# Weights converted from float64 at the start of a fused attention and feed-forward kernel: w_out and w3 in shared units, and the last output in two parts

## The chip, the cores and the metric

The kernel runs on one core of a Trainium2 chip. The metric is the device time of one execution in microseconds; the kernel before was run three times for it, and once more with the profiler on.

## What is computed

Random-feature attention over (8, 8, 576, 64) float32 inputs is followed by a bilinear feed-forward layer whose four weights are float64:

```
proj = x @ omega.T ;  phi(x) = exp(proj - |x|^2/2 - max) / sqrt(m)      # m = 128 features
kv = phi(k).T @ v ;  z = sum(phi(k)) ;  x = (phi(q) @ kv) / (phi(q) @ z)
out = ((x @ w1) * (x @ w2)) @ w3 @ w_out        # x (4608, 512), w1, w2 (512, 1024), w3 (1024, 1024), w_out (1024, 512)
```

## The kernel before, in words

**Chunks.** The 4608 tokens are 36 chunks of 128. Each chunk of keys and of queries is loaded, projected on the features by TensorE (`features`, L323 in float32 for the first key and query chunks, L330 with operands split in two float16 parts for the later ones), reduced to a maximum per head by VectorE (L342, `nm`), and put through exp by ScalarE (L354 or L357). The products of keys and values are summed by batch (`kv_batch`, L447), queries are attended (`q_attend`, L476), and the normalized rows `x` are transposed by a DMA. `gate` (L733) forms x @ w1 and x @ w2 in quarters of a group of chunks, multiplies them and splits the product in two float16 parts; `project_out` (L762 to L767) multiplies with W = w3 @ w_out, which is formed once at the start, scales by ScalarE (L766) and stores a chunk by one DMA of 256 KB (L767).

**Weights.** float64 weights come as pairs of 32-bit words and are converted on the chip in units of 1 MB, 128 partitions x 1024 numbers (`from_float64`). A unit is a list of five stages: `fetch` (a DMA into one of three raw buffers, L568), `magnitude` (ScalarE takes Abs of the upper words, L577), `bits` (VectorE makes float32 out of both words in four passes, L584 to L592), a product, and `keep`. For the first unit each stage works on two halves. Unit kinds, by their letter in `ORDER`: `o` is two blocks of 128 rows of w_out; `W` holds 256 columns of w3 transposed for 512 rows, and its product (L670) runs over four blocks j of w_out, for two output blocks k, in two PSUM banks; `keep` copies them to `Wb` (L685), or, for the second half of the rows, adds to it (L683). `1` and `2` are parts of w1 and w2, with column sums (L618, L622); `a`, `b` and `S` scale and split what is complete. A product of 128x128 by 128x512 in float32 is two records in the trace.

**What sets the order.** `ORDER` lists 25 units. Stage s of unit n is issued at tick n + SKEW[s] (0, 1, 2, 3, 5), and PER says how many ticks fall in a slot; the steps of the chunks (norms, scales, splits, k, q, attend, kv) are put in slots by tables of offsets (KOFF, QOFF, VB, KV_LAG and others). Each instruction's place in that list is its rank; the framework's scheduler takes ready instructions by rank when it builds the queues of the engines, and `early(kind, ...)` moves a step's rank forward by PR[kind] places (back, if negative). So a line of code that comes earlier isn't always first on its engine. `tc.issue_after(converted[-1])` puts an edge between the last pass of one unit and the passes of the next on VectorE; `converted[1]` also holds back the maxima of the first key chunk, and `converted[0]` and `converted[1]` some loads of v and q.

**Buffers.** TensorE writes to two PSUM pools: two double banks for projections, kv and nu (`banks`), and four single banks (`bank_m`) shared by the weight products, the column sums, the norms (L194), the gate and the output. Three raw buffers of 1 MB and two for magnitudes hold the units in work.

Of the kernel before, what the change touches and what calls it, by code (L numbers as in the profile page):

```python
# [9 lines left out]
F32 = mybir.dt.float32  # L10
# [9 lines left out]
P = 128  # L20
# [5 lines left out]
PASSES = ((0, 0), (0, 1), (1, 0))  # L26

F64_LEAST, F64_TOP = 2.0**-15, float.fromhex("0x1.dffffep+16")

# [3 lines left out]
QS = "a"  # L33
VS = "a"
WS = "a"
EH = 'aaaaaddadaaadaaaaaaaaaa'
EL = 'ddppddpdpddpppppppppppppppp'
QH = 'aaaaaaddd'
QL = 'ddpdppppppppppp'
DQ = '101110010000000000000000000'  # L40
QF = 6
KF = 11
VF = 9
V_ACT = 1
PR = {'vscale': 100, 'norm': 400, 'split': 100, 'bits': -100, 'x': 50}
START = 1
MS = 0
WADD = 1
FQ = 's'
T0 = 1  # L50
CH = 1
KFIRST = 0
QD = 1
OM1 = 0
DK = '1111111110000000000000'


ORDER = 'ooW1W1aW2W2booWWWW11a22bS'
SKEW = [0, 1, 2, 3, 5]

PER = [3, 1, 0, 1, 0, 1, 1, 0, 1, 0, 1, 1, 0, 1, 1, 0, 0, 1, 1, 1, 1, 1, 1, 1, 0, 3, 0, 1, 1, 1, 1, 1, 2]
# [13 lines left out]
OM_AT = 0  # L75
K_BEHIND = 1
RAW64_BUFS = 3
O_BUFS = 2
# [11 lines left out]
def tile_favor_attention_then_bilinear_ffn(  # L90
# [19 lines left out]
    nc = tc.nc  # L110
    NCH = qT.shape[0]
# [9 lines left out]
    DO = wo.shape[1] // 2  # L121
# [24 lines left out]
    def bank_m(name):  # L146
        return ps_m.tile([P, 512], F32, tag="pm", name=name)
# [398 lines left out]
    converted = []  # L546
# [8 lines left out]
    def from_float64(new, src, name, cuts=1):  # L555

        st = {}
        pieces = [slice(k, k + 1024 // cuts) for k in range(0, 1024, 1024 // cuts)]

        def fetch():  # L560
            at = st["at"] = raw_at.pop(0)
            nfetch[0] += 1
            raw = arena[:, at : at + 4].bitcast(U32).rearrange("p b i -> p (b i)")

            raw = raw.rearrange("p (j i) -> p j i", j=src.shape[1])
            step = src.shape[1] // cuts
            for k in range(0, src.shape[1], step):
                {'a': nc.scalar, 's': nc.sync, 'p': nc.gpsimd}[pick(FQ, nfetch[0])].dma_start(raw[:, k : k + step], src[:, k : k + step])  # L568
            st["raw"] = raw.rearrange("p j i -> p (j i)").rearrange("p (i t) -> p i t", t=2)

        def magnitude():

            at = st["mag"] = mag_at.pop(0)
            st["g"] = arena[:, at : at + 2].rearrange("p b i -> p (b i)")
            st["dst"] = new()
            for a in pieces:
                nc.scalar.activation(st["g"][:, a], st["raw"][:, a, 1].bitcast(F32), AF.Abs)  # L577

        def words():
            for a in pieces:  # L580
                g, dst = st["g"][:, a], st["dst"][:, a].bitcast(U32)
                top, low = st["raw"][:, a, 1], st["raw"][:, a, 0]

                nc.vector.tensor_scalar(g, g, F64_TOP, F64_LEAST, ALU.min, ALU.max)  # L584
# [71 lines left out]
    def W_block(n):  # L656

        i, j0 = n * 2 % NF, n * 2 // NF * HALF
        at = HALF + n % 2 * 2
        w3c = guest[:, at : at + 2].rearrange("p b i -> p (b i)")  # L660
        pss = []

        def product():
            w = w3c.rearrange("p (j i) -> p j i", j=HALF)
            for k in range(2):
                ps = bank_m(f"wp_{n}_{k}")
                if j0 and not WADD:
# [88 lines left out]
    def project_out(c):  # L756
        sc = oscs[:, c : c + 1]
        nc.vector.tensor_scalar(sc, pts[c], pts[c], kap, ALU.mult, ALU.mult)
        ps = bank_m(f"o_{c}")
        mm = [(f, a, b) for f in range(NF) for a, b in PASSES]  # L760
        for i, (f, a, b) in enumerate(mm):
            nc.tensor.matmul(ps, hs[c, f][0][:, a], W[f][:, b], start=i == 0, stop=i == len(mm) - 1)  # L762
        for f in range(NF):
            used(hs[c, f][1])
        o = mo.tile([P, DO], F32, tag="o", name=f"o_{c}", bufs=O_BUFS)
        nc.scalar.mul(o, ps, sc)  # L766
        nc.sync.dma_start(out[c * P : (c + 1) * P, :], o)  # L767


    LEAD = 5  # L770
# [20 lines left out]
    def unit(keep=0):  # L791
# [7 lines left out]


    make = {
        "o": wo_load,
        "W": W_block,
        "1": lambda i: w12_load(0, i),
        "2": lambda i: w12_load(1, i),
        "a": lambda i: [early("wsplit", lambda: w12_split(0, i))],
# [12 lines left out]
    for n, u in enumerate(units[:RAW64_BUFS]):  # L819
        u[0]()  # L820
        u[0] = None
        if START and n < 2:
            load(kT, n, "k", nc.scalar)
# [150 lines left out]
```

## Time and profile before

| | us |
|---|---|
| median of 3 runs (816.82 to 817.98) | 817.17 |
| the profiled execution's own time | 817.29 |
| its span in the profile | 815.5 |
| PE busy | 776.2 |
| DVE busy | 544.9 |
| ACT busy | 443.6 |
| POOL busy | 213.4 |

PE is TensorE, PEld its weight loads, DVE VectorE, ACT ScalarE, POOL GpSimd, SP the queue that issues most DMAs. The span is what the profiler saw of the program on the core; the time of a run has 1.8 us around it. A difference of 1 us is 0.12% of the time.

### The profile page before, as it was taken

The numbers are of one execution on the slowest core, as the hardware profiler recorded it, in microseconds if no ns is written. First come the engines' busy times: TensorE is split into PE (matmuls) and PEld (weight loads), VectorE is DVE, ScalarE is ACT, GpSimd is POOL, SyncE is SP. The second block draws the span as 40 slices with busy tenths as digits, with TensorE's granted clock in tenths as the row PEclk, the third lists the DMA queues.
The fourth block names the chain that finished last, engine by engine and source line by source line (L and its number), as shares of the span: only waits on it lengthen the run. The fifth ranks groups of instructions, "written<-read, shape, count | busy, mean of one in ns | idle before, by whom it ended". The sixth has DMA issues, their size and how long they took to land.

```text
span 815.5 us, 19863 instructions
## 1 busy us (share of the span) xinstructions
PE 776.2 (95%) x8320; PEld 578.9 (71%) x8320; DVE 544.9 (67%) x1045; ACT 443.6 (54%) x793; POOL 213.4 (26%) x208
## 2 busy tenths in 40 slices
PE   2998898998979999999999999999999999999998
PEld 2456557967758777777777778777777777777773
DVE  6898979867898686677767665686758654552210
ACT  4896667855766557566655555466545433332221
POOL 0000101121434243333332334333423321231110
PEclk9999999999999999999999999999999999999999
DMA  8787854233544364335434435254433342231101
GB/s 297 268 289 229 228 164 118 54 53 85 137 107 89 80 151 96 81 103 131 92 79 121 101 80 103 66 132 92 100 59 87 69 79 67 53 59 46 39 14 39
DMA packets 142537, 88.38 MB, mean 108 GB/s; under 512 B 116720, under 2 KB 116848, under 8 KB 142448
## 3 DMA queue, kind: packets, MB, share of 16 engines
q1 hardware_dynamic: 142160, 86.60, 42.0%
q8 instruction: 65, 1.06, 0.5%
q10 hardware_dynamic: 288, 0.52, 0.2%
q14 instruction: 24, 0.20, 0.1%
HBM read 49.35 MB, written 9.44 MB: 72 GB/s over the span
## 4 chain that ended last, share of the span: by engine, by line
PE 84%; DVE 6%; DMA 4%; ACT 3%; issue 2%; SPq 0%; ACTq 0%; DVEq 0%
PE ab L733 42%; PE o L762 21%; PE wp L670 7%; PE kvp L447 5%; PE nu L476 3%; PE qpj L330 2%; PE kpj L330 2%; DMA kraw<-kT 1%; DMA arena<-wo 1%; DVE nm L342 1%; DVE khl L175 1%; DMA arena<-w 1%; ACT qe L354 1%; DVE w12b L592 1%; DVE arena L589 1%
## 5 line engine op out<-in xcount | busy, mean ns | idle before, releaser
L733 PE MATMUL ab<-xT,w12b 128*128 128x256 f16 (+1 forms) x3840 | 393.9, 263 | 3.3 <-DMA xT<-xhl 2.7
L733 PEld LDWEIGHTS <-w12b 128*128 128x128 f16 x3840 | 341.8, 98 | 42.6 <-issue 3.2
L762 PE MATMUL o<-Wb,arena 128*128 128x512 f16 x864 | 192.4, 379 | 1.9 <-ACT asb L742 1.9
L748 POOL TENSOR_TENSOR arena<-asb,arena 128x512 f16<-128x512 f32 x72 | 84.7, 1176 | 279.8 <-ACT arena L747 272.7
L762 PEld LDWEIGHTS <-arena 128*128 128x128 f16 x864 | 82.1, 98 | 95.9 <-issue 2.0
L366 POOL TENSOR_TENSOR eq<-qe,eq 128x1024 f16<-128x1024 f32 x33 | 70.3, 2130 | 147.4 <-DVE eq L161 80.6
L743 DVE TENSOR_TENSOR asb<-ab,asb 128x512 f32<-128x512 f32 x72 | 49.5, 687 | 85.3 <-PE ab L733 71.9
L747 ACT CAST arena<-asb 128x512 f16<-128x512 f32 x72 | 44.3, 616 | 97.7 <-DVE asb L743 97.7
L366 POOL TENSOR_TENSOR ek<-ke,ek 128x1024 f16<-128x1024 f32 x25 | 53.3, 2130 | 87.7 <-ACT ek L163 87.1
L670 PE MATMUL wp<-w12b 128*128 128x512 f32 x128 | 62.9, 647 | 3.3 <-DVE w12b L592 3.3
L357 ACT ACTIVATE qe<-qe,ln_e,es 128x1024 f32<-128x1024 f32 x29 | 35.9, 1239 | 44.9 <-DVE qe L356 44.9
L742 ACT ACTIVATE asb<-ab 128x512 f32<-128x512 f32 x72 | 41.9, 582 | 20.1 <-PE ab L733 15.1
L357 ACT ACTIVATE ke<-ke,ln_e,es 128x1024 f32<-128x1024 f32 x25 | 31.0, 1240 | 39.5 <-DVE ke L356 39.4
L670 PEld LDWEIGHTS wp<-w12b 128*128 128x128 f32 x128 | 25.6, 207 | 34.2 <-issue 29.7
L175 DVE SCALAR_TENSOR_TENSOR qhl<-qraw,s,qhl 128x512 f16<-128x512 f32 x30 | 26.9, 898 | 33.2 <-ACT qhl L172 33.2
L513 DVE SCALAR_TENSOR_TENSOR xhl<-xs,p2r,xhl 128x512 f16<-128x512 f32 x36 | 28.3, 787 | 27.7 <-ACT xhl L512 27.5
L161 DVE CAST eq<-qe 128x1024 f16<-128x1024 f32 x30 | 21.2, 708 | 37.6 <-ACT qe L357 37.0
L766 ACT ACTIVATE o<-o,oscs 128x512 f32<-128x512 f32 x36 | 24.5, 680 | 37.8 <-PE o L762 37.8
L342 DVE TENSOR_REDUCE nm<-kpj 128x8 f32<-128x1024 f32 x36 | 43.8, 1219 | 1.2 <-PE kpj L330 0.6
L342 DVE TENSOR_REDUCE nm<-qpj 128x8 f32<-128x1024 f32 x36 | 43.8, 1217 | 0.2
L189 ACT ACTIVATE junk_q<-qraw 128x512 bf16<-128x512 f32 x30 | 18.8, 627 | 45.5 <-DMA qraw<-qT 45.5
L447 PE MATMUL kvp<-vhl,ek 128*128 128x65 f16 (+1 forms) x880 | 41.6, 208 | 1.2 <-DVE qe L356 1.0
(124 smaller groups left out, 923.9 us busy)
## 6 DMA issues: line engine op xcount, KB each, us to landing
vraw<-v SPq DMA_DIRECT2D x36, 256.0 KB, 3.8
qraw<-qT SPq DMA_DIRECT2D x36, 256.0 KB, 2.8
out<-o SPq DMA_DIRECT2D x36, 256.0 KB, 2.7
kraw<-kT SPq DMA_DIRECT2D x34, 256.0 KB, 3.1
arena<-w3T SPq DMA_DIRECT2D x8, 1024.0 KB, 5.3
arena<-w SPq DMA_DIRECT2D x8, 1024.0 KB, 5.9
arena<-wo SPq DMA_DIRECT2D x3, 1024.0 KB, 7.2
eqT<-eq SPq DMA_TRANSPOSE x72, 3.1
```

The lines of the kernel that those rows point to most:

```text
L175: nc.vector.scalar_tensor_tensor(lo, src, s, hi, ALU.mult, ALU.subtract)
L342: nc.vector.tensor_reduce(nm, pj, AX.X, ALU.max, negate=True)
L357: nc.scalar.activation(e, e, AF.Exp, scale=es, bias=ln_e)
L366: (nc.vector if lo == "d" else nc.gpsimd).tensor_tensor(t[:, 1], e, t[:, 0], ALU.subtract)
L447: nc.tensor.matmul(ps[:, h // 4, h % 4], x, y, start=n == 0, stop=n == len(mm) - 1)
L670: nc.tensor.matmul(ps, w[:, j, k * P : (k + 1) * P], guest[:, j], start=j == (0 if WADD else j0), stop=j == HALF - 1,)
L733: nc.tensor.matmul(ps[:, k], w12[m][i][cc][:, a, r * P : (r + 1) * P], x[:, b, cc, off : off + T], start=j == 0, stop=j == len(mm) - 1,)
L742: nc.scalar.mul(asb, ab[0], 2.0**-37)
L743: nc.vector.tensor_tensor(asb, ab[1], asb, ALU.mult)
L747: nc.scalar.copy(h[:, 0], asb)
L748: nc.gpsimd.tensor_tensor(h[:, 1], asb, h[:, 0], ALU.subtract)
L762: nc.tensor.matmul(ps, hs[c, f][0][:, a], W[f][:, b], start=i == 0, stop=i == len(mm) - 1)
```

## The change

The first four units are of a new kind, `F`. Unit j holds block j of w_out (512 KB) and, of w3 transposed, the same block of 128 rows with 512 columns (512 KB), fetched by two DMAs. Its product is four matmuls, one into each of the four single banks, opened by j = 0 and closed by j = 3; the `keep` of the last unit copies all four banks to Wb by ScalarE. So the four F units do what two `o` and two `W` units did. `ORDER` has the same number of units; the first two parts of w1 come one or two places later.

The first unit (CV 'C') is converted in another way: ScalarE scales the upper words (Copy) and makes the top three bits of the lower word out of one of its bytes (Identity), and VectorE needs three passes instead of four. CH = 4 makes each of the first four units wait on VectorE for the one before (it was 1: none).

The last chunk's output is formed in two halves of 256 columns, each with its own bank, matmuls, scaling and DMA (TAIL = 2).

Tables: the high part of query chunk 7 is made by ScalarE instead of VectorE (QH). Ranks (PR): `norm` from 400 to -50, `bits` from -100 to 0, `scale` 0 to 100, `mag` 0 to -20, `vsplit` 0 to 20. Offsets: VB[3] 2 to 3, QOFF[9] 0 to 1, KV_LAG 6 to 5. EH, EL, DQ and DK are longer, and choose the same for every chunk that reads them.

```
-QH = 'aaaaaaddd'
+QH = 'aaaaaadadddd'
-PR = {'vscale': 100, 'norm': 400, 'split': 100, 'bits': -100, 'x': 50}
+PR = {'vscale': 100, 'norm': -50, 'split': 100, 'x': 50, 'scale': 100, 'mag': -20, 'vsplit': 20}
+FKEEP = 'aaaa'
+OQ = 's'
+TAIL = 2
+CV = 'C0000000000000000000'
-CH = 1
+CH = 4
-ORDER = 'ooW1W1aW2W2booWWWW11a22bS'
+ORDER = 'FFFF1W1aW22booWWWW11a22bS'
-VB = {1: 0, 0: -1, 2: -1, 3: 2}
+VB = {1: 0, 0: -1, 2: -1, 3: 3}
-QOFF = {11: 2, 2: -1, 4: 1}
+QOFF = {11: 2, 2: -1, 4: 1, 9: 1}
-KV_LAG = 6
+KV_LAG = 5
...
# fetch
+            if isinstance(src, tuple):
+                for k, x in enumerate(src):
+                    q.dma_start(raw[:, 1024 * k : 1024 * (k + 1)], x)
...
# magnitude
-                nc.scalar.activation(st["g"][:, a], st["raw"][:, a, 1].bitcast(F32), AF.Abs)
+                if cv == "0":
+                    nc.scalar.activation(st["g"][:, a], top, AF.Abs)
...
+                else:
+                    nc.scalar.activation(st["g"][:, a], top, AF.Copy, scale=2.0**-112)
+                    low = st["raw"][:, a, 0]
+                    b3 = st["bytes"][:, a, 3]
+                    nc.scalar.activation(low, b3, AF.Identity, scale=2.0**-5, bias=third)
...
# words, kind C; the four passes of before stay for the other units
+                    nc.vector.tensor_scalar(g, g, F32_TOP, -F32_TOP, ALU.min, ALU.max)
+                    g = g.bitcast(U32)
+                    nc.vector.scalar_tensor_tensor(
+                        low, g, 3, low, ALU.logical_shift_left, ALU.bitwise_or
+                    )
+                    last = nc.vector.scalar_tensor_tensor(
+                        dst, g, 0x80000000, low, ALU.bitwise_and, ALU.bitwise_or
+                    )
...
+    def W_fore(j):
+        dst = w12b[:, 1, j : j + HALF + 1 : HALF]
+        def product():
+            if not fore:
+                fore.extend(bank_m(f"wf_{k}") for k in range(HALF))
+            for k, ps in enumerate(fore):
+                nc.tensor.matmul(
+                    ps,
+                    guest[:, HALF + j, k * P : (k + 1) * P],
+                    guest[:, j],
+                    start=j == 0,
+                    stop=j == HALF - 1,
+                )
+        def keep():
+            for k, ps in enumerate(fore):
+                copy(FKEEP[k] == "d", Wb[:, k + 1], ps)
+        src = (wo[j * P : (j + 1) * P], w3T[j * P : (j + 1) * P, 0 : 2 * HALF * P])
...
# project_out
+        cuts = TAIL if c == NCH - 1 else 1
+        for k in range(cuts):
+            d = slice(k * DO // cuts, (k + 1) * DO // cuts)
+            ps = bank_m(f"o_{c}_{k}")[:, 0 : DO // cuts]
+            for i, (f, a, b) in enumerate(mm):
+                nc.tensor.matmul(
+                    ps, hs[c, f][0][:, a], W[f][:, b, d], start=i == 0, stop=i == len(mm) - 1
+                )
+            nc.scalar.mul(o[:, d], ps, sc)
+            queue.dma_start(out[c * P : (c + 1) * P, d], o[:, d])
```

## Rows read from the trace of the kernel before

**Rows 1.** The profile page: the span, and busy time of each engine with its share and number of instructions.

```profile
span 815.5 us, 19863 instructions
PE 776.2 (95%) x8320; PEld 578.9 (71%) x8320; DVE 544.9 (67%) x1045; ACT 443.6 (54%) x793; POOL 213.4 (26%) x208
```

**Rows 2.** Busy time by stretches: the stretch and its length in us, then busy us and number of instructions of PE, PEld, DVE, ACT and POOL, the granted clock of TensorE (1 is full), the DMA engines' busy share and GB/s.

```profile
9.20:24.48 15.28, 2.08 (x16) 1.78 (x16) 14.81 (x21) 8.78 (x24) 0.00 (x0) 1.00 0.95 334
24.48:60.00 35.52, 35.52 (x112) 16.68 (x113) 31.59 (x48) 30.20 (x63) 0.00 (x0) 1.00 0.79 275
60.00:132.00 72.00, 63.14 (x539) 43.11 (x539) 63.70 (x109) 46.89 (x99) 5.38 (x9) 0.95 0.67 192
132.00:260.00 128.00, 118.84 (x1602) 97.87 (x1601) 105.01 (x197) 84.69 (x161) 36.58 (x41) 0.97 0.40 91
260.00:815.50 555.50, 551.70 (x6026) 415.29 (x6023) 327.04 (x658) 269.54 (x442) 169.99 (x146) 1.00 0.36 82
```

**Rows 3.** The timeline of PE alone, from the start to 260 us: start, length, line, operation, tile written and tiles read, shapes and number merged; in brackets the idle time before it and what ended it.

```profile
24.48 10.17 PE L670 MATMUL wp<-w12b 128*128 128x512 f32 x16 [1.21 <-DVE w12b L592]
34.49 0.59 PE L622 MATMUL l<-wab,ones_bf 128*128 128x512 bf16 x2
...
39.21 0.17 PE L194 MATMUL norm_v<-vam,ones_bf 128*128 128x8 bf16 x1
39.24 2.82 PE L670 MATMUL wp<-w12b 128*128 128x512 f32 x6
...
74.74 1.88 PE L323 MATMUL qpj<-om_raw,qraw 64*128 64x128 f32 x16 [3.59 <-ACT qe L354]
...
90.75 8.83 PE L670 MATMUL wp<-w12b 128*128 128x512 f32 x16 [2.07 <-DVE w12b L592]
...
200.91 5.34 PE L762 MATMUL o<-Wb,arena 128*128 128x512 f16 x24 [1.88 <-ACT asb L742]
```

**Rows 4.** The timeline of all engines in the first 30 us, in the same form: passes of the first units on ScalarE and VectorE, and the first product.

```profile
6.83 0.65 ACT L577 ACTIVATE arena<-arena 128x512 f32<-128x512 f32 x1
...
7.52 0.43 DVE L584 TENSOR_SCALAR arena<-arena 128x512 f32<-128x512 f32 x1 [0.21 <-ACT arena L577]
...
8.16 0.67 ACT L577 ACTIVATE arena<-arena 128x512 f32<-128x512 f32 x1 [0.67 <-DMA arena<-wo]
...
11.17 0.69 DVE L592 SCALAR_TENSOR_TENSOR w12b<-arena 128x512 uint32<-128x512 uint32 x1
...
12.05 0.69 DVE L584 TENSOR_SCALAR arena<-arena 128x1024 f32<-128x1024 f32 x1 [0.20 <-ACT arena L577]
...
13.53 1.14 ACT L577 ACTIVATE arena<-arena 128x1024 f32<-128x1024 f32 x1 [1.51 <-DVE arena L586]
...
15.92 2.35 DVE L342 TENSOR_REDUCE nm<-kpj 128x8 f32<-128x1024 f32 x2
...
24.48 6.31 PE L670 MATMUL wp<-w12b 128*128 128x512 f32 x7 [1.21 <-DVE w12b L592]
```

**Rows 5.** The chain of waits of the whole span, in order of time: start, length, what was waited for. The last row is its last step.

```profile
11.93 5.93 DMA arena<-w
...
43.59 7.06 PE wp L670 x16
...
811.78 0.69 ACT o L766
```

**Rows 6.** The timeline of VectorE from 30 to 165 us: its longest waits.

```profile
33.93 0.69 DVE L584 TENSOR_SCALAR arena<-arena 128x1024 f32<-128x1024 f32 x1 [3.31 <-ACT arena L577]
...
68.58 0.69 DVE L633 TENSOR_REDUCE l1m<-l 128x1 f32<-128x512 f32 x1 [1.49 <-PE l L622]
...
99.61 0.69 DVE L683 TENSOR_TENSOR Wb<-wp,Wb 128x512 f32<-128x512 f32 x1 [1.18 <-PE wp L670]
...
116.12 0.69 DVE L683 TENSOR_TENSOR Wb<-wp,Wb 128x512 f32<-128x512 f32 x1 [2.08 <-PE wp L670]
...
118.69 2.36 DVE L592 SCALAR_TENSOR_TENSOR w12b<-arena 128x1024 uint32<-128x1024 uint32 x2 [1.88 <-PE wp L670]
```

**Rows 7.** The DMAs that write `out` in the last 35 us: time from issue to landing.

```profile
DMA to landing us min/median/max: 2.0/2.0/2.0
```

**Rows 8.** Who waited for whom between 160 and 260 us: engine, tile and line, releaser, us in total, times, longest.

```profile
ACT junk_k L189 <- DMA kraw<-kT: 9.3, 4, 6.7
```

**Rows 9.** The timeline of all engines in a stretch of the steady part: squares of a query chunk, norm, a cast, the split, a projection, a quarter of the gate, the next norm.

```profile
592.57 0.63 ACT L189 ACTIVATE junk_q<-qraw 128x512 bf16<-128x512 f32 x1 [2.63 <-DMA qraw<-qT]
...
605.07 0.18 PE L194 MATMUL norm_q_k<-sums,ones_bf 128*128 128x3 bf16 x1
...
610.14 1.03 ACT L163 CAST ek<-ke 128x1024 f16<-128x1024 f32 x1
...
610.33 0.75 DVE L175 SCALAR_TENSOR_TENSOR khl<-kraw,s,khl 128x512 f16<-128x512 f32 x1
...
616.38 0.84 PE L330 MATMUL qpj<-om,qhl 64*128 64x128 f16 x24
...
617.16 5.41 PE L733 MATMUL ab<-xT,w12b 128*128 128x256 f16 x48
...
623.28 0.18 PE L194 MATMUL norm_q_k<-sums,ones_bf 128*128 128x3 bf16 x1
```

More of the change, by code (lines that the diff above doesn't have):

```diff
@@ L28 @@
 F64_LEAST, F64_TOP = 2.0**-15, float.fromhex("0x1.dffffep+16")
+F32_TOP = float.fromhex("0x1.dffffep-96")
 KS = "a"
@@ L35 @@
 WS = "a"
-EH = 'aaaaaddadaaadaaaaaaaaaa'
-EL = 'ddppddpdpddpppppppppppppppp'
-QH = 'aaaaaaddd'
+EH = 'aaaaaadadaaadaaaaaaaaaaaaa'
+EL = 'ddppddpdpddppppppppppppppppppp'
+QH = 'aaaaaadadddd'
 QL = 'ddpdppppppppppp'
-DQ = '101110010000000000000000000'
+DQ = '101110010000000000000000000000'
 QF = 6
@@ L54 @@
 OM1 = 0
-DK = '1111111110000000000000'
-ORDER = 'ooW1W1aW2W2booWWWW11a22bS'
+DK = '1111111110000000000000000000000'
+ORDER = 'FFFF1W1aW22booWWWW11a22bS'
 SKEW = [0, 1, 2, 3, 5]
@@ L157, in tile_favor_attention_then_bilinear_ffn @@
     nc.vector.memset(ln_e, 15 * math.log(2.0))
+    third = const.tile([P, 1], F32, name="third")
+    nc.vector.memset(third, -31.0 / 64)
     def copy(on_dve, dst, src):
@@ L563, in fetch @@
             raw = arena[:, at : at + 4].bitcast(U32).rearrange("p b i -> p (b i)")
[L565 to L569, printed above, removed]
+            q = {'a': nc.scalar, 's': nc.sync, 'p': nc.gpsimd}[pick(FQ, nfetch[0])]
+            if isinstance(src, tuple):
+                for k, x in enumerate(src):
+                    q.dma_start(raw[:, 1024 * k : 1024 * (k + 1)], x)
+            else:
+                to = raw.rearrange("p (j i) -> p j i", j=src.shape[1])
+                step = src.shape[1] // cuts
+                for k in range(0, src.shape[1], step):
+                    q.dma_start(to[:, k : k + step], src[:, k : k + step])
+            st["raw"] = raw.rearrange("p (i t) -> p i t", t=2)
+            st["bytes"] = raw.bitcast(mybir.dt.uint8).rearrange("p (i t) -> p i t", t=8)
         def magnitude():
@@ L576, in magnitude @@
             for a in pieces:
-                nc.scalar.activation(st["g"][:, a], st["raw"][:, a, 1].bitcast(F32), AF.Abs)
+                top = st["raw"][:, a, 1].bitcast(F32)
+                cv = st["cv"] = pick(CV, len(converted))
+                if cv == "0":
+                    nc.scalar.activation(st["g"][:, a], top, AF.Abs)
+                elif cv == "A":
+                    nc.scalar.activation(st["g"][:, a], top, AF.Abs, scale=2.0**-112)
+                else:
+                    nc.scalar.activation(st["g"][:, a], top, AF.Copy, scale=2.0**-112)
+                    low = st["raw"][:, a, 0]
+                    b3 = st["bytes"][:, a, 3]
+                    nc.scalar.activation(low, b3, AF.Identity, scale=2.0**-5, bias=third)
@@ L579, in words @@
         def words():
             for a in pieces:
-                g, dst = st["g"][:, a], st["dst"][:, a].bitcast(U32)
+                g, dst = st["g"][:, a], st["dst"]
                 top, low = st["raw"][:, a, 1], st["raw"][:, a, 0]
+                if len(dst.shape) == 2:
+                    dst = dst[:, a].bitcast(U32)
+                elif cuts == 2:
+                    dst = dst[:, a.start // 512].bitcast(U32)
+                else:
+                    dst = dst.bitcast(U32)
+                    g, top, low = (x.rearrange("p (k i) -> p k i", k=2) for x in (g, top, low))
@@ new lines, in words @@
+                if st["cv"] != "0":
+                    if st["cv"] == "A":
+                        g = g.bitcast(U32)
+                        nc.vector.tensor_scalar(g, g, 3, None, ALU.logical_shift_left)
+                        nc.vector.scalar_tensor_tensor(
+                            g, top, 0x80000000, g, ALU.bitwise_and, ALU.bitwise_or
+                        )
+                        last = nc.vector.scalar_tensor_tensor(
+                            dst, low, 29, g, ALU.logical_shift_right, ALU.bitwise_or
+                        )
+                        continue
+                    if st["cv"] == "C":
+                        nc.vector.tensor_scalar(g, g, F32_TOP, -F32_TOP, ALU.min, ALU.max)
+                    g = g.bitcast(U32)
+                    nc.vector.scalar_tensor_tensor(
+                        low, g, 3, low, ALU.logical_shift_left, ALU.bitwise_or
+                    )
+                    last = nc.vector.scalar_tensor_tensor(
+                        dst, g, 0x80000000, low, ALU.bitwise_and, ALU.bitwise_or
+                    )
+                    continue
@@ L693, in W_block @@
         ]
+    fore = []
+    def W_fore(j):
[10 more added lines that the diff above has]
+                    stop=j == HALF - 1,
+                )
+        def keep():
+            for k, ps in enumerate(fore):
+                copy(FKEEP[k] == "d", Wb[:, k + 1], ps)
+        src = (wo[j * P : (j + 1) * P], w3T[j * P : (j + 1) * P, 0 : 2 * HALF * P])
+        st = from_float64(lambda: dst, src, f"wf_{j}", cuts=1 if j or not START else 2) + [product]
+        return st + [early("keep", keep)] if j == HALF - 1 else st
     def W_split():
@@ L758, in project_out @@
         nc.vector.tensor_scalar(sc, pts[c], pts[c], kap, ALU.mult, ALU.mult)
-        ps = bank_m(f"o_{c}")
         mm = [(f, a, b) for f in range(NF) for a, b in PASSES]
-        for i, (f, a, b) in enumerate(mm):
-            nc.tensor.matmul(ps, hs[c, f][0][:, a], W[f][:, b], start=i == 0, stop=i == len(mm) - 1)
+        o = mo.tile([P, DO], F32, tag="o", name=f"o_{c}", bufs=O_BUFS)
+        queue = nc.scalar if pick(OQ, c) == "a" else nc.sync
+        cuts = TAIL if c == NCH - 1 else 1
[5 more added lines that the diff above has]
+                    ps, hs[c, f][0][:, a], W[f][:, b, d], start=i == 0, stop=i == len(mm) - 1
+                )
+            nc.scalar.mul(o[:, d], ps, sc)
+            queue.dma_start(out[c * P : (c + 1) * P, d], o[:, d])
         for f in range(NF):
             used(hs[c, f][1])
-        o = mo.tile([P, DO], F32, tag="o", name=f"o_{c}", bufs=O_BUFS)
-        nc.scalar.mul(o, ps, sc)
-        nc.sync.dma_start(out[c * P : (c + 1) * P, :], o)
     LEAD = 5
@@ L801, in tile_favor_attention_then_bilinear_ffn @@
     make = {
-        "o": wo_load,
-        "W": W_block,
+        "F": W_fore,
+        "o": lambda n: wo_load(n + 2),
+        "W": lambda n: W_block(n + 2),
         "1": lambda i: w12_load(0, i),
@@ L818, in tile_favor_attention_then_bilinear_ffn @@
         load(kT, c, "k")
-    for n, u in enumerate(units[:RAW64_BUFS]):
+    for n, u in enumerate([u for u in units if u[0]][:RAW64_BUFS]):
         u[0]()
```

## The prediction

> **What bounds the kernel now.** I read the page first, then the table by stretches, then the timelines. In the page PE is busy for 776.2 of 815.5 us [rows 1], so nearly every microsecond to be won is one of its 39.3 us of idle time. The stretches say where those lie [rows 2]: 3.8 us after 260 us, 9.2 us between 132 and 260, 8.9 us between 60 and 132, and 13.2 us between 9.20 and 24.48, where PE does one projection (2.08 us) while DVE is busy for 14.81 of 15.28 us. From 24.48 to 60 PE is never idle. So the change works on the largest hole, and the question is whether PE work moved into it stays gained, since DVE is busy for 63.7 of 72 us in the stretch after.
>
> The timeline of PE shows what ends the hole [rows 3]: the first products of weights (wp), 32 records in three runs from 24.48 to 42.06. They cannot start sooner, since a product of today's third unit needs all four blocks of w_out: units 0 and 1 (w_out) and 2 (w3) must be converted. DVE converts unit 0 by 11.86 and unit 1 by 15.9, then takes two maxima for the keys, then converts units 2 and 3; PE waits 1.21 us more for the last word of unit 2, until 24.48 [rows 3, 4].
>
> **The change, part by part.** *First products.* A unit now holds one w_out block and the w3 rows that meet it, so its product needs only itself. Unit 0: ScalarE's copy of the first half ends at 7.48, as its Abs does now; the new pass over a byte stands nowhere in the trace, nearest is the Abs of the same 128x512 elements, 0.65 us, which I take (bounds 0.6, somewhat under it, and 1.14, the Abs of twice as many). DVE spends 0.43 + 0.69 + 0.69 = 1.81 us on a half, the price of a pass with one operand and of two with two, and one of 0.43 goes [rows 4]. The second half lands at 8.16, ScalarE is done with it at 9.5, DVE at 11.4: 0.4 us sooner than 11.86, though DVE does 0.86 us less, since its last two passes wait for ScalarE. Bounds: 0.9 sooner to 0.6 later (both byte passes at the upper price). Unit 1 takes 3.9 us (12.05 to 15.92) and is ready at 15.3; the two maxima and their small follow-ups take 2.5 us; units 2 and 3, now strictly one after the other, are ready at 21.7 and 25.6. Data are no limit: the fourth fetch goes out when unit 0's buffer is free, 11.5, and lands 5.93 us later [rows 5], 17.5; ScalarE needs 1.14 us. A unit is now two fetches of 512 KB, so for the first three units SP issues six where it issued four; I allow 1 us for the two. ScalarE takes today's third unit at 13.53, when a magnitude buffer is free and not when data land [rows 4], and wants the new one near 16, so 2 us or more cover it.
>
> PE then: a product is 8 records. After a pause they last 0.90 us each (7 in 6.31 us from 24.48 on), later 0.44 (16 in 7.06) [rows 3, 5]: the lower of the two clock levels, 1.2 GHz, though the granted clock's column reads 1.00 there. Unit 0's product: 11.4 to 18.6. Unit 1's: to 22.1. The third projection of keys, half of its 2.08 at the higher level, to 23.2; unit 2's to 26.7; unit 3's to 30.3. Today the same work ends at 42.06, with 0.8 us of a column sum and a norm in between [rows 3]. **Head start: 42.06 - 0.8 - 30.3 = 11.0 us.**
>
> *What is late next.* The weights behind it keep their number and cost on DVE; DVE's conversions pace this stage, not PE. DVE can use the head start only where it waits for PE today: 1.49, 1.18, 2.08 and 1.88 us [rows 6], 6.6 us together, all behind long runs of products or of kvp. Its longest other idle, 3.31 us at 33.93, waits for a ScalarE pass that waits for a transfer, and stays. So I count **6.6 of the 11.0 us as kept**, with bounds 0 and 11.0, and 0.4 us for unit 0.
>
> *Four banks.* The products hold all four banks of the pool from 11.4 until ScalarE has copied them (4 x 0.65 us, as its pass over 128x512 [rows 4]), about 32.9. The first column sum is at 34.49 and the first norm of v at 39.21 [rows 3]; both come later than that: nothing. If unit 3's product came 10 us later, they would wait, and the splits of v behind them.
>
> *Last output in halves.* Today 0.69 us of ScalarE, an issue and a landing of 2.0 us follow the last matmul [rows 5, 7]. 48 matmuls of 256 columns take 5.41 us in a gate, 24 of 512 take 5.34 [rows 3, 9]: +0.07. ScalarE on 256 fewer columns: 0.25 less, half of the step between its forms of 512 and 1024 (0.65, 1.14 [rows 4]). Half the bytes save between 0 and 1.0 us (half of the landing): 0.3. Sum: **-0.5**.
>
> *Order edits.* One cast moves from DVE to ScalarE (1.03 us there [rows 9]) between 160 and 260, where DVE is busy for 0.82 and ScalarE for 0.66 of the time from 132 on [rows 2]: nothing (bounds -1 and +1). The squares for a scale lose rank (400 to -50), scale and v split gain. Between 160 and 260 ScalarE stands 9.3 us behind squares of keys alone whose chunk has not landed [rows 8]; moved back, they let other work pass. In the steady part the squares run 12.5 us ahead of their norm matmul (592.57, 605.07), and 450 places in a list of 552 per chunk (19863 / 36) at 18.2 us a chunk (605.07, 623.28) are an estimated 14.8 us: 2.3 too late, but the split ends 5.3 us before its projection (611.08, 616.38) [rows 1, 9], which covers it. I take nothing, with a gain of up to 4 us (under half of the 9.2 us) and a loss of up to 3.
>
> **Sum** against the profiled execution of 817.29 us (span 815.5 and 1.8 around it): 817.29 - 6.6 - 0.4 - 0.5 = 809.8. It lies 0.12 above the median of 817.17, so I forecast **809.7 us**.
>
> **Rivals.** *All of it is kept.* If PE, once ahead, finds gate products to do while DVE goes on, the sum has 11.0 for 6.6: 805.3, and with something from the order edits 803. For it: PE always has a backlog between 24.48 and 60. Against: in that stage its other work also comes from DVE. Chance 0.22.
>
> *Nothing is kept.* DVE's 6.6 us of idle time only moves, as each conversion waits instead for a buffer or a transfer (DMA share 0.95 between 9.20 and 24.48, 0.79 from there to 60 [rows 2]), or the change does not do what it says: the products are queued on PE behind the third projection and start near 21 us, or they come in short bursts and all run at the lower level, 32 x 0.90 = 28.8 us and 2.1 for the projection, from 11.4 to 42.3. In each of these no head start is left: 817.2 - 0.9 = 816.3, between 815 and 817.5. Chance 0.17, of it 0.05 for the bursts; against these, the sum above has no gap over 0.1 us among the four.
>
> *Slower: the clock.* PE's gaps of 3.59 and 2.07 us, the two long ones between 60 and 132, were each followed by work at half speed: 16 records took 8.83 us at 90.75 where they take 7.06, 1.77 us lost, and the granted clock of that stretch is 0.95, a tenth of it at 1.2 GHz, 3.6 us lost for the two. A gap of 1.88 us at 200.91 had no such price: 24 matmuls in 5.34 us, as ever [rows 2, 3, 5]. From 24.48 to 60 there is no gap now, because PE is the one behind. Take 11.0 us of backlog away and gaps of that sum appear between DVE's units, say five of 2.2 us; each lowers the clock, 5 x 1.77 = 8.8 us. If PE's lateness after a gap is then what DVE or the next exp waits for, none of the head start is kept and part of the 8.8 is lost besides: 816.3 + 4.4 = 820.7 with half of it, 825 with all. It decides from more than about 2.5 us unabsorbed (818.8). Against it: after a wait for DVE, PE is waited for by nobody as a rule. Chance 0.13.
>
> The Trainium skill, "TensorE: Matmul & The Clock Gate", section "HAM oscillation — how this bites in real kernels", speaks against this change in the same way: work in short bursts with waits between lets the clock fall again and again, and each burst starts slow. By that rule, taken strictly, the four products run slow as in the second rival, 816.3 in place of 809.7. The trace agrees with it for gaps of 2.07 us and more, not for the one of 1.88.
>
> **Numbers.** Forecast's case 0.48, all kept 0.22, nothing kept 0.17, slower 0.13. A measurement of this kernel can tell about 0.2% (1.6 us) from no change. Faster (under 815.5): the first two and 0.04 of the third, 0.74; within: 0.13; slower: 0.13. The range is 803 to 818: all kept with some gain of order, down to nothing kept with a small loss; out are most of the slower case (0.12) and 0.05 below.
>
> **What would show it.** Right: first product on PE near 11.4, 32 records done near 30, PE busy for 10 or more of the 15.3 us from 9.2, DVE's four waits for PE gone or short, PE's idle sum near 32, about 0.5 us less behind the last matmul. Wrong: the products start after 20, or all last 0.9 us; DVE's idle time before 130 us is as now, waiting for transfers; new gaps of PE between 30 and 60 followed by a granted clock of 0.83; ScalarE's squares late, with PE waiting for projections after 260.

## The result and the profile after

The changed kernel takes 824.24 us (median of 4 runs, 821.24 to 824.92) where the kernel before, beside it, takes 817.58 (4 runs): ratio 1.0066, interval 1.0044 to 1.0087. It is slower, by 6.7 us; I had forecast 7.5 us faster. The profiled execution of after took 824.74 us. The ratios below leave out three single executions far above the others (850.58 us in e3, 1611.11 in e2, and 843.51 in e5, which is its profiled one and of which little more than one run of matmuls is read).

The page of after, then the table by the same stretches as [rows 2]:

```profile
span 822.9 us, 19914 instructions
PE 781.7 (95%) x8344; PEld 583.2 (71%) x8344; DVE 560.0 (68%) x1043; ACT 447.5 (54%) x797; POOL 224.9 (27%) x208
```

```profile
9.20:24.48 15.28, 12.64 (x34) 5.87 (x35) 13.49 (x19) 8.83 (x19) 0.00 (x0) 1.00 0.87 304
24.48:60.00 35.52, 28.98 (x91) 13.70 (x90) 30.33 (x46) 28.20 (x64) 0.00 (x0) 0.86 0.83 284
60.00:132.00 72.00, 62.73 (x497) 42.35 (x496) 62.12 (x100) 47.21 (x102) 4.83 (x8) 0.91 0.66 193
132.00:260.00 128.00, 115.38 (x1588) 95.30 (x1586) 104.22 (x204) 85.75 (x161) 37.34 (x41) 0.99 0.44 92
260.00:822.90 562.90, 556.99 (x6111) 421.82 (x6108) 347.51 (x661) 273.36 (x448) 181.32 (x147) 1.00 0.37 81
```

The hole is filled as forecast: PE is busy for 12.6 us from 9.20 to 24.48, where it was 2.08. But the next stretch, in which it never stood still, now holds 6.5 us of idle time at a granted clock of 0.86, and from 60 to 132 us the clock is 0.91 for 0.95 [rows 2].

PE's timeline, to be read against [rows 3]: idle time in brackets, and how long the same number of matmuls takes after it. The rows wf are the products of the F units. W2, W3 and W4 are the third, fourth and fifth W unit of before, which keep their numbers in after, and the rows wp their products (W2 from 38.33, W3 from 50.66, W4 from 83.89 us); l is a column sum, kpj and qpj are projections of keys and queries, and kvp is the product of keys and values.

```profile
11.84 9.97 PE L756 MATMUL wf<-w12b 128*128 128x512 f32 x16 [2.94 <-DVE w12b L631]
...
28.25 3.70 PE L756 MATMUL wf<-w12b 128*128 128x512 f32 x8 [1.31 <-DVE w12b L643]
35.39 1.01 PE L673 MATMUL l<-wab,ones_bf 128*128 128x512 bf16 x2 [3.44 <-ACT wab L669]
36.33 2.07 PE L330 MATMUL kpj<-om_raw,kraw 64*128 64x128 f32 x14
38.33 6.11 PE L721 MATMUL wp<-w12b 128*128 128x512 f32 x10
...
50.66 8.83 PE L721 MATMUL wp<-w12b 128*128 128x512 f32 x16 [1.80 <-DVE w12b L643]
...
60.38 8.37 PE L454 MATMUL kvp<-vhl,ek 128*128 128x65 f32 x74
68.59 0.59 PE L673 MATMUL l<-wab,ones_bf 128*128 128x512 bf16 x2
...
76.38 2.08 PE L330 MATMUL qpj<-om_raw,qraw 64*128 64x128 f32 x16 [4.59 <-ACT qe L361]
79.39 2.08 PE L330 MATMUL kpj<-om_raw,kraw 64*128 64x128 f32 x16 [0.93 <-ACT ek L361]
83.89 7.21 PE L721 MATMUL wp<-w12b 128*128 128x512 f32 x10 [2.42 <-DVE w12b L643]
...
96.76 7.13 PE L721 MATMUL wp<-w12b 128*128 128x512 f32 x16 [0.37 <-DVE w12b L643]
```

At the full level 16 products take 7.13 us (the last row), so 10 take 4.46, and 16 projections 1.16. The 3.44 us gap at 31.95 costs the column sum, the projection and the first ten products of W2 some 0.4 + 1.0 + 1.65 us over their length at the full level; the gap of 1.80 costs W3 1.70; those of 4.59 and 2.42 cost 0.92 twice and 2.75. Together 9.4 us at the lower level, beside the gaps. The 1.31 us gap cost nothing. Against before, W2 starts 5.2 us earlier (38.33 against 43.52), W3 1.4 earlier, kvp 0.3 later, W4 7.3 later, the first gate product 5.5 later.

VectorE's waits from 24 to 100 us (line waited for, us in total, times, longest):

```profile
DVE l1m L684 <- PE l L673: 5.0, 2, 4.8
DVE arena L635 <- ACT arena L593: 3.9, 4, 2.7
DVE gd L492 <- PE nu L483: 2.6, 1, 2.6
DVE total L205 <- PE norm_v L201: 1.6, 1, 1.6
```

I had expected the waits for PE in [rows 6] to go. They grew: the three rows for PE make 9.2 us, where the kernel before has 2.9 in the same stretch. VectorE's busy time up to 100 us is 78.2 us, where it was 85.4: it does 7 us less work by then, although PE's products began 12.6 us earlier. The wait of 2.7 us is for ScalarE, whose queue holds three of the four new copies of the first products ahead of the pass waited for, among other work:

```profile
33.31 1.07 ACT L170 COPY Wb<-wf 128x512 f32<-128x512 f32 x2
34.26 1.08 ACT L669 ACTIVATE wab<-w12b 128x1024 bf16<-128x1024 f32 x1
35.21 2.15 ACT L361 ACTIVATE ek<-kpj,nm 128x128 f32<-128x128 f32 x8
37.22 1.16 ACT L593 ACTIVATE arena<-arena 128x1024 f32<-128x1024 f32 x1
```

The pass at 37.22 is the seventh unit's; VectorE takes it up at 38.41. And the chain behind the last matmul is shorter, with landings of 1.7 us for the halves of the last output (2.0 before [rows 7]):

```profile
804.21 15.62 PE o L844 x96
...
819.85 0.47 ACT o L847
```

```profile
out<-o SPq DMA_DIRECT2D x2, 128.0 KB, 1.7
```

### The profile page after: what moved, and what is told of

Its sections match the earlier page's. It is cut to its first block, busy times and chain, and to the rows that moved or that the text cites. A ratio compares the mean times of both kernels' runs of the same rounds, so it can differ in the third digit from the quotient of the medians.

```text
span 822.9 us, 19914 instructions
## 1 busy us (share of the span) xinstructions
PE 781.7 (95%) x8344; PEld 583.2 (71%) x8344; DVE 560.0 (68%) x1043; ACT 447.5 (54%) x797; POOL 224.9 (27%) x208
## 4 chain that ended last, share of the span: by engine, by line
PE 64%; DVE 4%; ACT 4%; DMA 3%; issue 2%; SPq 0%; ACTq 0%; DVEq 0%
PE ab L810 37%; PE o L844 18%; PE kvp L454 3%; PE nu L483 2%; PE qpj L337 2%; DMA kraw<-kT 2%; PE kpj L337 2%; DVE nm L349 1%; DVE asb L820 1%; DVE khl L182 1%; DVE qe L363 1%; DMA xT<-xhl 1%; ACT ek L170 1%; DVE ke L363 0%; ACT qhl L179 0%
## 5 line engine op out<-in xcount | busy, mean ns | idle before, releaser
L810 PEld LDWEIGHTS <-w12b 128*128 128x128 f16 x3840 | 338.3, 98 | 45.3 <-issue 4.5
L844 PE MATMUL o<-Wb,arena 128*128 128x512 f16 (+1 forms) x888 | 192.8, 373 | 1.4 <-ACT asb L819 1.4
L844 PEld LDWEIGHTS <-arena 128*128 128x128 f16 x888 | 84.9, 98 | 95.1 <-issue 1.5
L373 POOL TENSOR_TENSOR eq<-qe,eq 128x1024 f16<-128x1024 f32 x33 | 82.1, 2486 | 157.5 <-DVE eq L168 87.2
L364 ACT ACTIVATE qe<-qe,ln_e,es 128x1024 f32<-128x1024 f32 x29 | 36.0, 1240 | 52.5 <-DVE qe L363 52.5
L721 PE MATMUL wp<-w12b 128*128 128x512 f32 x96 | 48.8, 667 | 4.6 <-DVE w12b L643 4.6
L847 ACT ACTIVATE o<-o,oscs 128x512 f32<-128x512 f32 (+1 forms) x37 | 24.7, 667 | 38.9 <-PE o L844 38.9
L519 ACT ACTIVATE xhl<-xs,p2r 128x512 f16<-128x512 f32 x36 | 25.8, 716 | 28.5 <-DVE p2r L225 28.3
L483 PEld LDWEIGHTS <-eqT 128*128 128x128 f16 (+1 forms) x960 | 31.8, 101 | 13.3 <-issue 6.2
L182 DVE SCALAR_TENSOR_TENSOR khl<-kraw,s,khl 128x512 f16<-128x512 f32 x25 | 37.6, 1505 | 4.5 <-ACT khl L179 3.9
L721 PEld LDWEIGHTS wp<-w12b 128*128 128x128 f32 x96 | 19.9, 214 | 29.1 <-issue 23.1
```

The costliest lines, as they stand in the source:

```text
L182: nc.vector.scalar_tensor_tensor(lo, src, s, hi, ALU.mult, ALU.subtract)
L373: (nc.vector if lo == "d" else nc.gpsimd).tensor_tensor(t[:, 1], e, t[:, 0], ALU.subtract)
L483: nc.tensor.matmul(nu[r0:r1, h // 4, h % 4], t[:, x, place(h), r0:r1], kvs[b][:, y, h], start=n == 0, stop=n == 2,)
L721: nc.tensor.matmul(ps, w[:, j, k * P : (k + 1) * P], guest[:, j], start=j == (0 if WADD else j0), stop=j == HALF - 1,)
L810: nc.tensor.matmul(ps[:, k], w12[m][i][cc][:, a, r * P : (r + 1) * P], x[:, b, cc, off : off + T], start=j == 0, stop=j == len(mm) - 1,)
L844: nc.tensor.matmul(ps, hs[c, f][0][:, a], W[f][:, b, d], start=i == 0, stop=i == len(mm) - 1)
```

## The experiments

A ratio is always to the kernel before, run beside it. Theory of the clock: the gaps that the head start leaves on PE are followed by work at 1.2 GHz, and that, with what waits for it, is the loss. Rivals: the new ranks; the new offsets; VectorE's queue.

**Undoing one part each.** e1 has the F units alone (PR, the offsets, CV, TAIL of before); e2 all but the F units; e3 and e4 undo one part of after:

```
e1: PR, VB, QOFF, KV_LAG, QH of before; CV = '0'; TAIL = 1
e2: ORDER = 'ooW1W1aW2W2booWWWW11a22bS'; CH = 1
e3: PR = {'vscale': 100, 'norm': 400, 'split': 100, 'bits': -100, 'x': 50}
e4: VB, QOFF, KV_LAG, QH of before
```

> The kernel before with the F units and their edge (CH = 4) alone: ranks, offsets, first conversion and last output as before. Theory 1 (the head start that the F units win, 32 records done at 32 us in place of 42, is lost again between 32 and 130 us, since TensorE gets gaps there, falls to the lower clock, and VectorE waits behind it): slower than before by about 5 us, 822 to 825, with a granted clock near 0.86 between 24.5 and 60. Theory 2 (the changed ranks cost the time, the F units bring what was predicted): 809 to 812. Theory 3 (the offsets cost it): 809 to 812 as well.

> The changed kernel with the order of units of before (o o W 1 W 1 a ...) and no edge among the first four; ranks, offsets, first conversion and halved last output as changed. Theory 1: about as before less the tail, 816 to 818. Theory 2 or 3: slower than before by 5 us or more, 822 to 829.

> The changed kernel with the ranks of before (norm 400, bits -100, no scale, mag, vsplit). Theory 1: still slow, 821 to 826. Theory 2 (ranks): 809 to 813.

> The changed kernel with VB, QOFF, KV_LAG and QH of before. Theory 1: still slow, 821 to 826. Theory 3 (offsets): 809 to 813.

| | us | ratio, interval |
|---|---|---|
| e1, F alone | 830.04 | 1.0144, 1.0125 to 1.0163 |
| e2, all but F | 821.16 | 1.0040, 1.0021 to 1.0060 |
| e3, old ranks | 831.07 | 1.0141, 1.0120 to 1.0162 |
| e4, old offsets | 821.61 | 1.0038, 1.0026 to 1.0049 |

The F units alone cost 12 us, more than I had thought any of their gaps could. The ranks are the opposite of a cause: without them the changed kernel is 6 us slower. The offsets cost about 2.3 us (1.0066 less 1.0038, though the two intervals overlap). Of the four forecasts only that of e4 held: e1 and e3 came out above their bands by 5 us, and e2 at 821.16 lies between its two, 816 to 818 and 822 to 829. In e1 the clock fell most behind 60 us, and ahead of it less than expected (0.90 from 24.48 to 60, for 0.86). PE in e1:

```profile
60.86 1.01 PE L673 MATMUL l<-wab,ones_bf 128*128 128x512 bf16 x2 [2.16 <-ACT wab L669]
61.82 15.59 PE L454 MATMUL kvp<-vhl,ek 128*128 128x65 f32 x72
77.35 2.08 PE L330 MATMUL qpj<-om_raw,qraw 64*128 64x128 f32 x16
```

One gap of 2.16 us, and the whole run of kvp, 72 matmuls without a gap, goes at the lower level: 15.59 us, where after has 74 in 8.37. The projections behind it are still slow. From 60 to 132 us the granted clock is 0.74 (0.91 in after). e3, after with the old ranks, has the same gap in the same place, and that is what the new ranks take away:

```profile
59.39 0.84 PE L673 MATMUL l<-wab,ones_bf 128*128 128x512 bf16 x2 [2.81 <-ACT wab L669]
60.35 15.59 PE L454 MATMUL kvp<-vhl,ek 128*128 128x65 f32 x72
```

**e5 and e6: keep PE busy through a part of a gap.** Products with a zero matrix are added into the open bank: 12 ahead of e1's gap, 8 behind the last F product of after. No other instruction changes its place in any queue. ZERO stands for the lower halves of a float32 identity matrix read as bfloat16, which are all zero, and ZERO4 for four of them side by side; the traces show them as `ident`.

```
e5, column sum of unit (1, 0):
+            for x in range(12):
+                nc.tensor.matmul(l1s[n, i], ZERO, ab[:, 0], start=False, stop=False)
e6, W_fore.product, j == HALF - 1:
+            for x in range(8):
+                nc.tensor.matmul(fore[-1], ZERO, ZERO4, start=False, stop=x == 7)
```

> The kernel of e1 (F units alone) with 12 products by a zero matrix put into an open column-sum bank, ahead of the gap of 2.16 us on TensorE at 58.7; no other instruction moves, and the sums stay the same. Clock theory: the gap is what drops TensorE to 1.2 GHz, and the kvp run behind it (15.6 us for 72 records) stays there; with the gap filled it takes some 8.4 us, the kernel 820 to 824 in place of 830. Pacing theory (VectorE's and ScalarE's work sets the time, the clock is a symptom): 829 to 831.

> The changed kernel with 8 products by a zero matrix behind the last F product, 1.7 us into the gap of 3.44 us at 31.95; nothing else moves. Clock theory: the products of unit 5 run at 2.4 GHz and end 2 to 3 us sooner, the wait of VectorE for the norm of v (1.56 us) goes: 820 to 822.5 in place of 824. Pacing theory: 823.5 to 825.

e5: 822.54 us, 1.0077 (1.0044 to 1.0109), for 1.0144 without: 12 useless products take about 5.5 us off. The nine executions lie in two groups, six from 818.78 to 822.62 us and three from 828.69 to 829.84, as slow as e1; what kvp did in those three no trace shows. From the trace:

```profile
55.78 2.87 PE L677 MATMUL l<-wab,ident 128*128 128x512 bf16 x12
...
61.96 8.28 PE L454 MATMUL kvp<-vhl,ek 128*128 128x65 f32 x72 [0.36 <-ACT ek L361]
```

It starts at 61.96, as in e1 (61.82), and takes 8.28 us for 15.59. So the lower level, and no wait, made the difference of these two. The fill shortened the gap ahead of the column sum, from 2.16 to 1.52 us; it did not close it. e6: 821.88 us, 1.0048 (1.0030 to 1.0067), for 1.0066: in the forecast band, though the intervals overlap. Its fill covered a part of the gap only, 2.08 us were left, and the gap of 1.80 ahead of W3 stayed. W2's ten products take 5.27 us for 6.11, and VectorE's wait for the norm of v behind them is 0.7 us for 1.6.

**e7: VectorE's queue.** In after the column sum's reduction (69.22 us) waits 4.8 us for PE, and the last pass of the eleventh unit (70.49 us) is behind it. The rank of the splits of w1 and w2 is moved back so that it no longer is:

```
-PR = {..., 'mag': -20, 'vsplit': 20}
+PR = {..., 'mag': -20, 'vsplit': 20, 'wsplit': -25}
```

> The changed kernel with the rank of the steps that scale w1 and w2 set back by 25, so that the maximum of column sums no longer stands on VectorE's queue ahead of the last pass of unit 10 (a wait of 4.79 us at 64.4 in the changed kernel, for column sums that are queued behind kvp on TensorE). Queue theory (VectorE loses what the F units won by waiting in order for TensorE): 818 to 821. Clock theory alone: 823 to 825.

830.16 us, 1.0151 (1.0128 to 1.0174): the forecast failed. The other order put a gap of 3.55 us where e1 had one:

```profile
62.16 14.98 PE L454 MATMUL kvp<-vhl,ek 128*128 128x65 f32 x72 [3.55 <-ACT ek L361]
```

The wait for the column sum is gone from VectorE's list, but it now waits 9.7 us for what follows the slow kvp. So this run tells nothing of the queue by itself, and no other run takes that wait away: the queue stays an open rival. e7 shows a second time what a gap ahead of kvp costs.

**e8 and e9: the small parts.** e8 is the kernel before with the last output in halves; e9 is after with the first unit converted as the others are.

```
e8, before: TAIL = 2          e9, after: CV = '0'
```

> The kernel before with the halved last output alone. All theories: 0.5 to 0.8 us faster than before, so 817.1 to 817.4 against 817.9; the changed kernel has 3.1 us behind its last matmul where before has 3.8.

> The changed kernel with the first unit converted as all others are (VectorE's two-sided clamp and masks instead of ScalarE's pass over a byte); nothing else in any queue's order changes. My prediction gave this part 0.4 us of gain. The changed kernel's profile has the first unit's two halves ready as early as the sum said, so by that theory this kernel is 0 to 0.6 us slower than the changed kernel: 824.2 to 824.8. Rival, that the byte pass on ScalarE is what holds the transfers or the second unit back: 821 to 823.5. Theory of the clock: the first product enters about as early either way, no difference.

e8: 818.24 us, 1.0003 (0.9988 to 1.0018). e9: 822.62 us, 1.0060 (1.0038 to 1.0083), for 1.0066; its time lies in the rival's band, but the kernel before took 817.07 beside it, and the ratio is that of after. Neither part can be told from nothing.

**e10 to e12: put it together.** All have the offsets of before and e6's 8 products. e10 has 12 more at W4's start; e11 adds `FKEEP = 'dddd'`; e12 is e10 with 6 more at W3's start and 6 at W4's behind the last projection:

```
e10, W_block.product, n == 4, k == 0:
+                for x in range(12):
+                    nc.tensor.matmul(ps, ZERO, ZERO4, start=x == 0, stop=False)
e12, n == 3: 6 of these; n == 4: the 12, and
+                with tc.issue_after(lastk[-1].ins):
+                    for x in range(6):
+                        nc.tensor.matmul(ps, ZERO, ZERO4, start=False, stop=False)
```

> The changed kernel with the four offsets of before (821.6 us as measured), and beside that 8 products with a zero matrix behind the last of the first four units' products and 12 more behind W4's start, in the bank that W4 opens: TensorE is busy through the gap ahead of l at 34.2 and the one ahead of W4 at 83.7, and nothing is late for it. Clock theory: W2's first 10 products (5.72 us) and W4's first 10 (7.03 us) go back towards 4.46 each, 1.3 and 2.5 us, and what comes after is up to that much earlier: 818 to 820.5. If the lower clock in these stretches is not what delays the rest (VectorE sets the pace): 821 to 822.

> As the run with two fills, and the four copies of the finished first products go to VectorE instead of ScalarE. ScalarE was busy 9.4 of the 10 us from 30 to 40 us, and the Abs pass of the seventh unit, which VectorE waited 2.7 us for, stood behind these copies. Theory that ScalarE's queue makes the new wait: l and the seventh unit come 2 to 3 us earlier, the gap ahead of l shrinks, 816 to 819. Rival, VectorE paces this stage and four copies are four more of its passes: units 6 to 9 not earlier, 820 to 824.

> As the run with two fills, which came out even with the kernel before (818.6 against 817.1 us), and beside that 6 products with a zero matrix at W3's start, in the 1.80 us gap ahead of W3, and 6 at W4's start, issued only behind the kpj that ends ahead of W4's 2.43 us gap (the 12 of the last run stay, where they ran, ahead of qpj). No instruction of the kernel itself moves in its queue. Clock theory: W3 takes 7.1 instead of 8.83 us, 1.7 earlier, and W4's first 10 products 4.5 to 5.5 instead of 7.03, at most 2.5 earlier: 814.5 to 817.5, so even with the kernel before or just faster. If behind the third gap VectorE and not TensorE sets the pace, W4's end is not earlier and the run is where the last one was, 818 to 819.

e10: 818.63 us, 1.0011 (0.9992 to 1.0029): even with before, for 1.0038 without fills.

A part of PE's wait ahead of W2 is for a load of keys, whose landing differs between executions. In e4, then in e10:

```profile
36.97 1.63 PE L330 MATMUL kpj<-om_raw,kraw 64*128 64x128 f32 x14 [2.22 <-DMA kraw<-kT]
```

```profile
31.83 1.96 PE L769 MATMUL wf<-ident 128*128 128x512 bf16 x8
34.09 0.59 PE L673 MATMUL l<-wab,ones_bf 128*128 128x512 bf16 x2 [0.30 <-ACT wab L669]
35.73 1.16 PE L330 MATMUL kpj<-om_raw,kraw 64*128 64x128 f32 x14 [1.05 <-DMA kraw<-kT]
36.82 4.56 PE L726 MATMUL wp<-w12b 128*128 128x512 f32 x10
...
47.60 8.83 PE L726 MATMUL wp<-w12b 128*128 128x512 f32 x16 [1.80 <-DVE w12b L643]
...
80.82 7.03 PE L726 MATMUL wp<-w12b 128*128 128x512 f32 x10 [2.43 <-DVE w12b L643]
```

W2's ten products take 4.56 us (5.72 in e4), as the clock theory says. W3 starts 2.88 us earlier than in e4 (50.48 there). Of these, 1.24 us are the load of keys, which lands earlier in this execution, and 1.64 the projection and the ten products at the higher level. The 12 for W4 ran ahead of qpj, not in W4's gap, so W4 stayed at 7.03 us and that half of the expectation was not met; W4 too starts 2.87 us earlier, so nothing was won between W3 and W4, and the time came from ahead of W3. e11: 820.31 us, 1.0036 (1.0022 to 1.0050), in the band of the rival, not the 816 to 819 of the theory that ScalarE's copies make the wait. The four copies take VectorE 0.69 us each among the sixth unit's passes, and W2 starts at 39.50 us there, 36.82 in e10. But the load of keys lands 1.8 us later than in e10 and a second projection runs ahead of W2, so the trace does not show that the copies make W2 late. e12: 817.23 us, 1.0006 (0.9990 to 1.0022), in its band, and not told from e10 or from before.

```profile
37.38 6.25 PE L732 MATMUL wp<-w12b 128*128 128x512 f32 x10
...
49.86 7.13 PE L732 MATMUL wp<-w12b 128*128 128x512 f32 x16
...
81.44 4.96 PE L732 MATMUL wp<-w12b 128*128 128x512 f32 x10
...
92.07 7.13 PE L732 MATMUL wp<-w12b 128*128 128x512 f32 x16 [0.37 <-DVE w12b L644]
...
100.18 2.91 PE L825 MATMUL ab<-xT,w12b 128*128 128x128 f16 x49 [0.34 <-DMA xT<-xhl]
```

Here W3 and W4 go at the full level or nearly, but W2's ten products take 6.25 us, behind the same 8 fills with which they take 4.56 in e10. So no traced run holds the full level in W2, W3 and W4 at once, and what the head start would be worth then is not shown. The first gate product is at 100.18 us, where it was at 99.41 before. With most of the clock held up the kernel is no longer slower, and of the head start nothing is left.

## Why the prediction was wrong

**The head start: right.** The first product starts at 11.84 (11.4 forecast), the 32 records end at 31.95 (30.3). Of 11.0 us forecast, 9.3 came (41.26 less 31.95).

**"6.6 of the 11.0 us as kept": the step that failed.** It took VectorE's waits for PE as time that an earlier PE frees. They lie behind long runs (column sum behind kvp, kvp behind W3, W3 behind a unit of VectorE's own), and these runs start when VectorE has converted the next unit, which is hardly earlier: the W3 unit's conversion ends at 50.61 us for 51.88 before, 1.3 us of a head start of 9.3. The last pass of that unit, in after and before:

```profile
49.39 1.22 DVE L643 SCALAR_TENSOR_TENSOR w12b<-arena 128x1024 uint32<-128x1024 uint32 x1
```

```profile
50.66 1.22 DVE L592 SCALAR_TENSOR_TENSOR w12b<-arena 128x1024 uint32<-128x1024 uint32 x1
```

So the waits came back, larger. The runs put what is kept at about 0 when a part of the clock is given back (e10, e12: 1.0011 and 1.0006, first gate product 0.8 us later than before in e12), not 6.6, and at less than that when it is not. In both, VectorE still waits 4.8 us (e10) and 3.8 (e12) for column sums, 1.5 before; how much of the missing 6.6 us that wait takes stays open, since e7 was the only run on it.

**The clock.** The rival "slower: the clock" (0.13) names what happened, at 820.7 to 825 us forecast and 824.24 measured, but the number is in part luck. Its five gaps of 1.77 us each stand against 9.4 us at the lower level, so that size was near. Yet of the 6.7 us lost some 2.3 are the offsets', and the fills give back 2.2 us (e10 against e4, by the ratios) and 2.6 (e12), where the rival counted 4.4 to 8.8. What I set against it, that PE after a wait for VectorE is waited for by nobody as a rule, was wrong: VectorE waits 4.8 us for the column sum queued behind kvp and 1.6 for the norm of v behind W2. kvp itself runs at the full level there, so the first of these waits is the clock's only by the 1.70 us that W3 loses ahead of it. e5 shows by insertion alone that the lower level costs e1 its time; for after itself the times of e4 and e12 say the same, of a smaller part (the intervals of these two do not overlap, those of e4 and e10 just do). That the sum has no gap over 0.1 us among the four first products was wrong by a gap of 1.31 us, which had no price; and I had not followed the list past them, to the column sum's wait for ScalarE. The rule of the Trainium skill, "TensorE: Matmul & The Clock Gate", section "HAM oscillation — how this bites in real kernels", that bursts with waits between start slow again and again, agrees with this case in part: the runs behind the gaps of 2.42, 3.44 and 4.59 us started slow, and W3 behind 1.80 us fell to the lower level about 1 us after its start. The 96 gate matmuls behind 2.67 us in e10 and the product behind 1.31 us ran at full speed.

**Order edits at nothing, -4 to +3:** two large terms were hidden in it, and without the F units these edits, with the tail and unit 0's conversion, cost 3.3 us (e2). The offsets cost about 2.3 us (e4): after has two gaps on PE that e4's trace lacks and e2's has (1.44 us at 315.30, 1.16 at 325.95):

```profile
320.53 0.16 PE L201 MATMUL norm_q_k<-sums,ones_bf 128*128 128x3 bf16 x1 [1.67 <-ACT asb L819]
...
331.18 3.80 PE L454 MATMUL kvp<-vhl,ek 128*128 128x65 f16 x120 [1.16 <-DVE ke L363]
```

The ranks are worth about 6 us to the changed kernel (1.0141 less 1.0066), by keeping the gap away from kvp. e2, all but F, lies at 1.0040, so most of its loss may well be the offsets'; no run has the new ranks without the F units and without the offsets. The cover of 5.3 us for late squares was misread: the split at 610.33 [rows 9] is of keys and the projection at 616.38 of queries, and the keys' own projection comes later still, at 622.51.

**Four banks:** the copies themselves freed the banks in time, by 38.8 (32.9 forecast), ahead of the norm of v at 44.27, but I had not counted what they delay on ScalarE: three of them, 1.65 us, stand ahead of the passes at 34.26 and 37.22. In e11 VectorE was no better place.

**The tail:** 3.08 us behind the last matmul for 3.76, -0.7 where -0.5 was forecast; too small for the time to show (e8). **Unit 0 by ScalarE:** ready at 11.78, forecast 11.4, with data 0.3 us later; nothing in the time (e9), so no run shows the 0.4 us of the sum.

The account, in ratios: after 1.0066; offsets back 1.0038; fills besides 1.0011. What is left cannot be told from no change.

## What to carry to other kernels

Work moved into a hole takes away the backlog that covered later waits: before counting a head start as kept, follow the same instruction list past the hole and see whose conversion, copy or sum each following run waits for. A gap on TensorE, where it is paid for at all, is priced by what runs next: here 0.9 us ahead of 16 small projections, 1.7 ahead of 16 large products, 7 ahead of the long run of kvp. When a change to the order gains less than it should, products with a zero matrix in the gaps, placed so that no queue changes, tell the clock from the order of the queues; loads that land at other times have to be taken out of the traces by hand, and the medians of many runs compared.

## What the runs showed of the hardware

A run of 72 float32 matmuls of 65 columns without a gap stayed at the lower level to its end: 15.59 us at a granted clock of 0.50 throughout (e1), and 14.98 in e7, where the clock is 0.62 over the first 2.84 us and 0.50 from there on. 10 to 16 products of 512 columns came back to the full level within the run: 8.83 us for 16, with 7.13 at full and an estimated 14.3 if all were slow. W3 in after shows it, with a granted clock of 1.00 at its start, 0.50 from 52.5 to 54.5 us and 1.00 from 55.5. The column misses some slow work, though: in after it reads 1.00 from 11.84 to 19.00 us, where the first 16 products take 9.97 us for 7.13.

The same gap does not always have the same price. Ahead of the same 96 gate matmuls, e10 and e12:

```profile
134.62 5.52 PE L819 MATMUL ab<-xT,w12b 128*128 128x128 f16 x96 [2.67 <-DMA xT<-xhl]
```

```profile
133.19 7.15 PE L825 MATMUL ab<-xT,w12b 128*128 128x128 f16 x96 [2.70 <-DMA xT<-xhl]
```

The twelve runs of e12 lie between 814.85 and 821.78 us, and its profiled one took 821.06, with a granted clock of 0.95 from 132 to 260 us where e10's had 0.99. One trace therefore does not settle a term of 2 us; where a trace and a median differ, the argument above goes by the median.

VectorE is busy for 560 us with the new ranks and for 545 with the old, at the same 1043 instructions (after, e3). Single passes take longer; of the split of keys, in after and in e3 (times, busy us, mean ns):

```profile
L182 DVE SCALAR_TENSOR_TENSOR khl<-kraw,s,khl 128x512 f16<-128x512 f32 x25 | 37.6, 1505 | 4.5 <-ACT khl L179 3.9
```

```profile
L182 DVE SCALAR_TENSOR_TENSOR khl<-kraw,s,khl 128x512 f16<-128x512 f32 x25 | 23.2, 927 | 0.6 <-ACT khl L179 0.6
```

The traces show what goes with it, two passes that start together in after:

```profile
328.25 1.74 DVE L182 SCALAR_TENSOR_TENSOR khl<-kraw,s,khl 128x512 f16<-128x512 f32 x1 [0.18 <-ACT khl L179]
328.28 1.16 POOL L825 TENSOR_TENSOR arena<-asb,arena 128x512 f16<-128x512 f32 x1
```

In after, 20 of the 25 splits run beside a tensor pass of GpSimd and take 1.44 to 2.62 us; the other five take 0.74 or 0.75. In e3 five run beside one, at 1.64 to 1.71 us, and 20 beside none, at 0.74 or 0.75. So the new ranks bring the two engines' passes together, and these passes make 14.4 of the 15 us. Whether it costs the kernel time is not shown.
